# A fused attention and ReGLU block: half of one more norm transposed by DMA, one load moved forward, and a new order of steps

## The chip, the cores and the metric

The kernel runs on one core of a Trainium2 chip. The core has a matrix engine (PE, with its weight loads shown as PEld), a vector engine (DVE), a scalar engine (ACT), a small-work engine (POOL) and a queue engine (SP) that here only issues DMAs. Sixteen DMA engines move data. Each compute engine takes its instructions in the order in which the program lists them for it, and an instruction that needs another engine's result waits for a semaphore. The metric is the device time of one execution in microseconds, lower is better.

## What is computed

One transformer block on 2048 positions of 512 channels, in bf16:

```python
x = A_x
h = x + _A_ref(_layernorm(x, axis=-1), A_wqkv, A_wo)
h2 = h + _B_ref(_layernorm(h, axis=-1), B_W_gate, B_W_up, B_W_down)
```

`_A_ref` is attention with 32 heads of 16 channels. Each position looks at 8 earlier positions, 2 apart, its own included: q, k, v from `wqkv`, logits, softmax over the 8, weighted sum of v, product with `wo`. `_B_ref` is a gated layer with 1376 hidden channels: `relu(x W_gate) * (x W_up)`, then `W_down`. The norms have no weights.

## The kernel before

The positions are cut into 4 chunks of 512, each of 4 blocks of 128. For each chunk the kernel adds small steps to a plan: a step has an engine, an assumed duration, dependencies, the buffers that it takes, and a function that issues its instructions. The steps of one chunk are, in short:

- first norm: statistics of each block on DVE (`xst`, L420, and `xag`, L423), two small functions on ACT for the inverse deviation (`xrl`, L433, and `xre`, L437), the normalized row on DVE (`xxn`, L455, a tile `row`, of which there are 5), and its transpose into the chunk's tile `quad` (9 of them). A transpose is either four matmuls against an identity on PE (`xtp`, L484) followed by an eviction on ACT (`xte`, L500) or on DVE (`xtv`, L498), or one DMA transpose issued by SP (`xtd`, L473). The table `DMAT` lists which pairs of blocks go by DMA: `('h',2,0)` means second norm, chunk 2, the pair that begins at block 0. Chunk 0's first norm goes block by block.
- q, k and v: 12 steps of 4 matmuls of 128x512 (`qkv`, L525), evicted by ACT (L533). In chunk 0 the first four q/k steps are cut into halves of 256 columns (`qka` needs blocks 0 and 1, `qkc` all four).
- scores: 4 products of q with shifted k on DVE (`pr`, L572, 2.2 us each), summed by PE (`sc0` and `sc1`, L578), exponential on ACT (`ex`, L594), a mask on DVE in chunk 0 (L597), the sum over the 8 positions on PE (L611) and its inverse on ACT (L614, L617).
- weighted sum: attention weights spread by PE (`bc`, L639) and evicted by ACT (`be`, L645), 4 products with shifted v on DVE (`mu`, L660, 2.2 us each), summed in trees. In chunks 0 to 2 the first level of a tree is an accumulating DMA issued by POOL (L692), the others are on DVE (L663, L667, L686).
- output projection on PE (`wo`, L712; in chunk 0 the residual is added by PE too, L715), residual sum (L721 on ACT in chunk 0, L723 on DVE elsewhere), squares on ACT (`hsq`, L409), second norm with the same kinds of transposes (`htp`, `hte`, `htd`).
- gated layer: `mm`, L750, on PE; L754 and L757 on ACT; L770 on DVE; `dn`, L787, on PE; the last sum on DVE (L798), and the store issued by SP (L802).

What sets the order: `RANK` holds one number for each step, in the order in which steps are added. `Plan.order` sorts each engine's steps by that number. So every engine's list, SP's included, is fixed by `RANK` alone; a start time that the planner works out from assumed durations and assumed landing times (`load(...)`) decides which free buffer a step gets, and in what sequence the engines' lists are written out. No step overtakes another on its engine, on the chip either.

Loads are issued in `setup()`: x of chunk 0 in four pieces and the q/k weights in four pieces, by SP and ACT in turn; then x of chunk 1, the v weights, x of chunks 2 and 3, `wo`, `W_up`, `W_gate` and `W_down`, all by SP. Between them stand small copies on POOL into the next load's destination. Such a copy reads something that an earlier load brings, so the next load, which overwrites the copied element, is issued only after that earlier load has landed. Before PE has data it runs 44 small matmuls on a cleared tile (L374) and later 16 more (L382).

Of the kernel before, what the change touches and what calls it, by code (L numbers as in the profile page):

```python
# [15 lines left out]


RANK = [
    0, 1, 2, 3, 4, 5, 6, 7, 8, 9, 10, 11, 12, 13, 14, 15, 16, 18, 19, 24,
    26, 31, 32, 17, 20, 22, 23, 25, 29, 34, 35, 28, 33, 37, 39, 41, 45, 48, 21, 27,  # L20
    30, 36, 38, 42, 44, 46, 63, 74, 40, 56, 68, 49, 51, 54, 43, 60, 72, 53, 66, 65,
    77, 70, 83, 75, 80, 90, 92, 87, 114, 102, 110, 85, 105, 93, 104, 115, 125, 129, 78, 88,
    95, 99, 103, 183, 193, 202, 132, 143, 150, 156, 152, 106, 109, 116, 123, 119, 168, 181, 216, 220,
    224, 180, 188, 217, 223, 231, 187, 196, 226, 229, 234, 162, 172, 201, 205, 207, 237, 240, 239, 245,
    247, 251, 242, 248, 243, 246, 252, 256, 259, 263, 250, 254, 265, 266, 272, 278, 269, 276, 285, 275,
    283, 273, 280, 286, 318, 322, 292, 301, 304, 314, 313, 324, 341, 311, 325, 298, 303, 334, 338, 326,
    330, 346, 354, 360, 337, 355, 317, 353, 347, 358, 370, 329, 352, 340, 348, 332, 345, 294, 350, 356,
    361, 374, 343, 365, 372, 381, 351, 362, 413, 357, 368, 367, 386, 418, 400, 425, 460, 464, 417, 427,
    457, 467, 376, 434, 446, 466, 410, 429, 437, 668, 55, 61, 52, 57, 50, 58, 47, 59, 62, 64,
    67, 84, 73, 82, 86, 71, 81, 69, 79, 89, 166, 175, 122, 136, 111, 130, 137, 190, 91, 101,  # L30
    127, 173, 149, 179, 94, 96, 163, 213, 158, 170, 98, 107, 108, 167, 208, 197, 249, 257, 244, 235,
    255, 260, 264, 268, 274, 296, 279, 302, 309, 305, 310, 307, 287, 295, 290, 293, 300, 319, 328, 364,
    369, 315, 320, 359, 363, 335, 342, 380, 382, 327, 336, 373, 375, 389, 395, 387, 392, 396, 402, 393,
    399, 398, 401, 397, 403, 405, 409, 404, 407, 411, 412, 416, 419, 420, 423, 421, 428, 422, 426, 431,
    474, 482, 441, 443, 458, 463, 453, 468, 483, 438, 448, 436, 452, 442, 451, 450, 454, 456, 488, 492,
    479, 498, 455, 487, 491, 500, 507, 461, 493, 445, 459, 481, 485, 471, 475, 496, 511, 539, 524, 533,
    520, 535, 526, 530, 541, 514, 540, 484, 502, 543, 544, 556, 581, 589, 538, 552, 559, 562, 549, 554,
    584, 587, 529, 547, 560, 564, 113, 120, 100, 124, 76, 117, 97, 112, 128, 133, 140, 144, 142, 146,
    164, 145, 154, 148, 157, 161, 209, 230, 174, 186, 198, 200, 195, 215, 182, 184, 199, 228, 189, 211,
    169, 177, 178, 194, 232, 241, 271, 281, 185, 191, 261, 253, 284, 297, 289, 282, 308, 312, 321, 331,  # L40
    339, 344, 378, 366, 377, 371, 379, 383, 385, 394, 388, 391, 390, 430, 439, 470, 490, 424, 432, 473,
    476, 440, 447, 486, 489, 406, 415, 465, 477, 501, 518, 497, 504, 508, 512, 494, 499, 521, 525, 517,
    519, 516, 522, 503, 505, 527, 528, 532, 546, 534, 537, 536, 548, 531, 542, 579, 597, 566, 594, 585,
    601, 561, 580, 609, 599, 603, 588, 592, 571, 575, 577, 600, 605, 606, 610, 595, 623, 602, 611, 582,
    614, 627, 558, 576, 574, 578, 568, 572, 565, 567, 583, 621, 648, 639, 645, 636, 649, 591, 616, 652,
    624, 635, 628, 633, 640, 655, 663, 665, 667, 632, 654, 661, 711, 650, 656, 707, 710, 644, 657, 659,
    669, 126, 138, 118, 134, 131, 139, 121, 135, 141, 147, 155, 160, 151, 171, 159, 165, 153, 176, 203,
    236, 218, 225, 192, 204, 214, 219, 258, 291, 262, 270, 222, 233, 267, 277, 227, 238, 212, 221, 288,
    316, 206, 210, 306, 299, 323, 333, 384, 349, 408, 414, 433, 435, 444, 462, 449, 506, 510, 509, 513,
    515, 469, 495, 478, 472, 480, 563, 570, 586, 593, 523, 551, 557, 569, 573, 590, 596, 598, 545, 550,  # L50
    553, 555, 615, 622, 604, 607, 612, 619, 608, 613, 626, 629, 618, 620, 630, 631, 617, 625, 634, 637,
    638, 641, 646, 653, 643, 651, 642, 647, 691, 695, 681, 692, 694, 698, 688, 697, 700, 679, 687, 674,
    677, 670, 680, 666, 671, 690, 673, 675, 672, 682, 658, 662, 660, 678, 683, 684, 689, 664, 685, 699,
    702, 676, 693, 705, 701, 706, 704, 709, 686, 703, 708, 713, 715, 716, 718, 696, 714, 719, 720, 722,
    724, 731, 712, 726, 732, 734, 717, 725, 727, 730, 728, 733, 735, 737, 721, 723, 729, 736,
]


# [33 lines left out]
class Plan:  # L92
# [9 lines left out]
    def add(self, key, *a, **k):  # L102
        op = Op(*a, **k)
        op.key = key
        op.seq = len(self.ops)
        if RANK:
            op.prio = RANK[op.seq]
        self.ops.append(op)
        for b in set(op.take) | set(op.use):
            b.left += 1  # L110
        return op
# [76 lines left out]
def kernel(  # L188
# [11 lines left out]
    nc = tc.nc  # L200
# [4 lines left out]
    NT = D // P  # L205
# [11 lines left out]
    BPC = CS // P  # L217
# [4 lines left out]
    x_rows = A_x.rearrange("b (tb p) d -> p (b tb) d", p=P)  # L222
# [20 lines left out]
    x_sm = sb.tile([P, NTB, D], BF16, name="x_sm")  # L243
    wqk_sb = sb.tile([P, NT, 2 * D], BF16, name="wqk_sb")
    wv_sb = sb.tile([P, NT, D], BF16, name="wv_sb")
# [32 lines left out]
    def setup():  # L278
# [3 lines left out]
            (nc.scalar if j % 2 else nc.sync).dma_start(x_sm[:, j:j + 1, :], x_rows[:, j:j + 1, :])  # L282
        for dt in range(NT):
            (nc.scalar if dt % 2 else nc.sync).dma_start(wqk_sb[:, dt:dt + 1, :], w3_r[:, dt:dt + 1, 0:2 * D])
        nc.scalar.preload_act_table_set("natural_log_exp_and_others")
        V.memset(warm[:], 0.0)
        make_identity(nc, identity[:])
# [7 lines left out]
        nc.gpsimd.memset(vT[:, :, 0:PADL], 0.0)  # L295


        nc.gpsimd.tensor_copy(out=x_sm[0:1, BPC, 0:1], in_=x_sm[0:1, 0, 0:1])
        nc.sync.dma_start(x_sm[:, BPC:2 * BPC, :], x_rows[:, BPC:2 * BPC, :])
        nc.gpsimd.tensor_copy(out=wv_sb[0:1, 0, 0:1], in_=wqk_sb[0:1, NT - 1, 0:1])  # L300
        nc.sync.dma_start(wv_sb[:], w3_r[:, :, 2 * D:3 * D])
        nc.gpsimd.tensor_copy(out=x_sm[0:1, 2 * BPC, 0:1], in_=x_sm[0:1, BPC, 0:1])
        for tk in range(2, NCK):
# [32 lines left out]
    DAL = 5.5  # L336
    TDD, TDL = 1.25, 1.5
    NWARM, NFILL = 44, 8
    DMAT = (('h',2,0),('h',2,2),('x',3,0),('x',3,2),('h',3,0),('h',3,2),('h',1,0))

    EARLY = (1, 2, 3)

# [20 lines left out]
    def load(t):  # L363
        return add(None, "LD", 0.0, None, lat=t)

    xload = [[load(t) for t in (3.4, 3.4, 4.2, 4.2)]] + [[load(t)] * BPC for t in (9.5, 14.0, 15.5)]
    wload = {n: load(t) for n, t in
             (("q", 8.0), ("k", 8.0), ("v", 12.0), ("o", 17.5), ("u", 21.5), ("g", 25.5), ("d", 29.5))}

    wb = Buf(bank_s)  # L370

# [14 lines left out]
    def layernorm(tk, src, dst_slots, pr, groups, on_act, residual=None):  # L386
# [7 lines left out]
        for grp in groups:  # L394
# [72 lines left out]
            for j0 in range(lo, hi, step):  # L467
                if (ln, tk, j0) in DMAT:
                    for j in range(j0, min(j0 + step, hi)):
# [38 lines left out]
    for tk in range(NCK):  # L508
# [143 lines left out]
        for t in range(NT):  # L652
# [18 lines left out]
            if (tk, t) in PESUM:  # L671
                u = Buf(od_s)
# [66 lines left out]
        for f0 in range(0, NFT, 2):  # L739
# [3 lines left out]
            for ft in fts:  # L743
# [20 lines left out]
                d = add(("ge%d" % (f0 // 2), tk), "ACT", A5, f_ge, [c], pr - 200, take=[gr], use=[gm], lat=AL)  # L764
# [50 lines left out]
    with tc.manual_schedule():  # L815
        setup()
        for op in todo:
            if op.fn is not None:
                op.fn()
# [35 lines left out]
```

The softmax here doesn't subtract the row's maximum and nothing guards it: scores larger than these inputs give would overflow.

## Time and profile before

| | |
|---|---|
| median of 13 runs | 203.53 us (202.96 to 204.83) |
| the profiled execution | 203.53 us, of which the span of the profile is 201.6 us |
| granted PE clock | 0.999 of full speed |
| step of one 128x512 matmul, start to start | 0.216 us |
| DVE, product of q and k or of weights and v (128x4096) | 2.28 us, 32 of them |
| DVE, statistics of one block | 0.67 us, 16 of them |
| ACT, one eviction of 128x512 | 0.60 to 0.64 us |
| ACT, eviction of two transposed blocks (128x1024) | 1.03 us, 7 of them |
| SP, issue of one DMA transpose | 1.20 to 1.86 us, 14 of them; landing 2.4 to 4.9 us after the issue begins |
| x of one chunk (512 KB), issue to landing | 6.1 us (median of three) |

How to read the profile: its times run from the span's start. An instruction's busy time can overlap the next one's on the same engine, since the engines are pipelined; from start to start they stand a little closer than the busy time says. A row of the timeline gives the start, the time from the first start to the last end of the instructions merged in it, engine, line, operation, tiles and shape, and in brackets how long the engine was idle before it and which instruction or transfer ended that.

### The profile page before, as it was taken

Reading aid. Unit: us, or ns where it says so; the run is one execution under the profiler, and the core shown is the slowest. Engines: PE = TensorE matmul, PEld = TensorE weight load, DVE = VectorE, ACT = ScalarE, POOL = GpSimd, SP = SyncE. Lnnn points to the kernel's source line nnn. Section 1 sums busy time; section 2 is a strip of 40 time slices with the busy share of each in tenths; the row PEclk is TensorE's granted clock in tenths of the full one; section 3 lists DMA queues with packets and bytes.
Section 4 is the critical chain, followed back from the end, with each engine's and each line's share of the span. In section 5 each row is a group of like instructions: output and inputs, shape, how many; then the busy total and the mean of one; then the engine's idle time right before and its main releaser. Section 6 shows DMA issues by size and latency. Waiting matters only on the chain.

```text
span 201.6 us, 2940 instructions
## 1 busy us (share of the span) xinstructions
PE 193.8 (96%) x1095; PEld 96.3 (48%) x1115; DVE 153.2 (76%) x239; ACT 122.0 (61%) x256; POOL 12.9 (6%) x29
## 2 busy tenths in 40 slices
PE   8799999989999999999999999999999999999993
PEld 8686446545445434444444444444444444444452
DVE  6688999999999999999996958799967422122313
ACT  3358699746899966787536679801556731277500
POOL 4000000330000004100122000000000000000000
PEclk9999999999999999999999999999999999999999
DMA  5779971897000008930199600131010050200103
GB/s 150 266 235 393 402 232 29 157 201 137 3 0 0 0 3 156 189 71 3 29 179 194 147 3 0 26 78 52 3 52 0 0 104 3 78 0 0 52 0 104
DMA packets 17676, 18.81 MB, mean 93 GB/s; under 512 B 8352, under 2 KB 14464, under 8 KB 17664
## 3 DMA queue, kind: packets, MB, share of 16 engines
q1 hardware_dynamic: 15360, 11.57, 18.4%
q0 software_dynamic: 1728, 6.29, 16.8%
q10 hardware_dynamic: 576, 0.79, 1.5%
q8 instruction: 8, 0.13, 0.3%
q14 instruction: 4, 0.03, 0.1%
HBM read 8.42 MB, written 2.10 MB: 52 GB/s over the span
## 4 chain that ended last, share of the span: by engine, by line
PE 54%; DVE 24%; DMA 11%; ACT 5%; issue 2%; SPq 1%; POOL 0%; DVEq 0%; ACTq 0%; POOLq 0%
PE bank L750 29%; PE bank L787 14%; DMA x_sm<-in_A_x_dram 7%; DVE big L572 7%; DVE big L660 7%; PE bank L525 6%; PE bank L712 5%; DMA quad<-row 4%; DVE st L420 2%; DVE row L455 2%; DVE gT L770 2%; DVE x_sm L723 1%; DVE big L663 1%; ACT big L645 1%; ACT row L409 1%
## 5 line engine op out<-in xcount | busy, mean ns | idle before, releaser
L750 PE MATMUL bank<-quad,wu_sb 128*128 128x512 bf16 (+1 forms) x172 | 42.4, 379 | 0.4
L750 PE MATMUL bank<-quad,wg_sb 128*128 128x512 bf16 (+1 forms) x173 | 42.0, 379 | 0.3 <-DMA quad<-row 0.3
L757 ACT ACTIVATE gr<-bank 128x512 bf16<-128x512 f32 (+1 forms) x44 | 25.3, 616 | 24.7 <-PE bank L750 22.9
L787 PE MATMUL bank<-wd_sb,gT 128*128 128x512 bf16 (+2 forms) x183 | 39.8, 366 | 0.2
L754 ACT CAST up_sb<-bank 128x512 bf16<-128x512 f32 (+1 forms) x44 | 25.0, 600 | 21.0 <-PE bank L750 17.3
L572 DVE TENSOR_TENSOR big<-quad,kT 128x4096 bf16<-128x4096 bf16 x16 | 36.2, 2283 | 0.1
L660 DVE TENSOR_TENSOR big<-big,vT 128x4096 bf16<-128x4096 bf16 x16 | 35.9, 2282 | 0.0
L770 DVE TENSOR_TENSOR gT<-gr,up_sb 128x1024 bf16<-128x1024 bf16 (+1 forms) x24 | 15.3, 643 | 24.0 <-ACT up_sb L754 14.4
L525 PE MATMUL bank<-quad,wqk_sb 128*128 128x512 bf16 (+1 forms) x139 | 30.2, 355 | 1.9 <-DMA wqk_sb<-in_A_wqkv_dram 0.9
L787 PEld LDWEIGHTS <-gT 128*128 128x128 bf16 (+1 forms) x187 | 18.1, 98 | 19.6 <-issue 0.4
L750 PEld LDWEIGHTS <-wg_sb 128*128 128x128 bf16 (+1 forms) x176 | 17.3, 100 | 21.2 <-issue 0.9
L750 PEld LDWEIGHTS <-wu_sb 128*128 128x128 bf16 (+1 forms) x176 | 17.5, 100 | 20.6 <-issue 0.7
L525 PEld LDWEIGHTS <-wqk_sb 128*128 128x128 bf16 x144 | 15.5, 114 | 13.9 <-issue 2.2
L798 DVE TENSOR_TENSOR row<-x_sm,bank 128x512 bf16<-128x512 bf16 (+1 forms) x17 | 10.6, 650 | 10.4 <-PE bank L787 10.4
L645 ACT CAST big<-bank 128x512 bf16<-128x512 f32 x32 | 17.7, 635 | 0.3 <-PE bank L639 0.2
L663 DVE TENSOR_TENSOR big<-big 128x1024 bf16<-128x1024 bf16 (+2 forms) x24 | 16.8, 728 | 0.1
L692 POOL DMA_DIRECT2D big<-big x12 | 10.5, 875 | 87.7 <-DVE big L660 59.8
L525 PE MATMUL bank<-quad,wv_sb 128*128 128x512 bf16 x62 | 15.6, 380 | 0.2
L712 PE MATMUL bank<-wo_sb,quad 128*128 128x512 bf16 x62 | 15.2, 379 | 0.2
L455 DVE TENSOR_SCALAR row<-x_sm,mv,rs 128x512 bf16<-128x512 bf16 x32 | 11.4, 408 | 3.1 <-ACT rs L437 3.1
L500 ACT COPY quad<-bank 128x1024 bf16<-128x1024 bf16 (+1 forms) x9 | 8.0, 932 | 6.8 <-PE bank L484 6.8
L533 ACT CAST quad<-bank 128x512 bf16<-128x512 f32 x16 | 9.4, 608 | 4.5 <-PE bank L525 4.5
(69 smaller groups left out, 147.5 us busy)
## 6 DMA issues: line engine op xcount, KB each, us to landing
big<-big POOLq DMA_DIRECT2D x12, 512.0 KB, 5.3
out_dram<-row SPq DMA_DIRECT2D x15, 128.0 KB, 1.8
x_sm<-in_A_x_dram SPq DMA_DIRECT2D x3, 512.0 KB, 6.1
wu_sb<-in_B_W_up_dram SPq DMA_DIRECT2D x1, 1376.0 KB, 9.3
wg_sb<-in_B_W_gate_dram SPq DMA_DIRECT2D x1, 1376.0 KB, 12.3
wd_sb<-in_B_W_down_dram SPq DMA_DIRECT2D x1, 1280.0 KB, 16.4
wqk_sb<-in_A_wqkv_dram ACTq DMA_DIRECT2D x2, 256.0 KB, 6.6
wqk_sb<-in_A_wqkv_dram SPq DMA_DIRECT2D x2, 256.0 KB, 6.7
```

The source lines that it names most:

```text
L455: V.tensor_scalar(out=xn.t[:], in0=x, scalar1=mv.t[:, j, 0:1], scalar2=rs.t[:, j:j + 1], op0=ALU.add if residual else ALU.subtract, op1=AL ...
L525: nc.tensor.matmul(mm.t[:, lo:hi], lhsT=wv_sb[:, dt, t:D:NT] if c == 2 else wqk_sb[:, dt, c * D + t:(c + 1) * D:NT], rhs=xnT.t[:, dt, lo:h ...
L572: V.tensor_tensor(out=pb.t[:].rearrange("p (t w) s -> p t w s", t=2), in0=q4, in1=k4, op=ALU.mult)
L645: nc.scalar.copy(out=ab.t[:, w, :], in_=bc.t[:])
L660: V.tensor_tensor(out=mt.t[:], in0=ab.t[:], in1=v8, op=ALU.mult)
L663: V.tensor_tensor(out=mt.t[:, 0:n, :], in0=mt.t[:, 0:n, :], in1=mt.t[:, n:2 * n, :], op=ALU.add)
L712: nc.tensor.matmul(od.t[:], lhsT=OT.t[:, t, j * P:(j + 1) * P], rhs=wo_sb[:, t, :], start=(t == 0), stop=(t == NT - 1 and tk not in RPE))
L750: nc.tensor.matmul(mm.t[:fs, :], lhsT=w_sb[:, dt, ft * P: ft * P + fs], rhs=hnT.t[:, dt, :], start=(dt == 0), stop=(dt == NT - 1))
L754: nc.scalar.copy(out=ub.t[:fs, i, :], in_=um.t[:fs, :])
L757: nc.scalar.activation(out=gr.t[:fs, i, :], in_=gm.t[:fs, :], func=ACT.Relu)
L770: V.tensor_tensor(out=gt.t[:fs, 0:n, :], in0=gr.t[:fs, 0:n, :], in1=ub.t[:fs, 0:n, :], op=ALU.mult)
L787: nc.tensor.matmul(od.t[:, c0:c1], lhsT=gts[ft].t[:fs, ft % 2, j * P:(j + 1) * P], rhs=wd_sb[:fs, ft, c0:c1], start=(ft == 0), stop=(ft == ...
```

## The change

1. `DMAT` gets `('x',2,2)`: in the first norm of chunk 2, blocks 2 and 3 are transposed by DMA (two more issues on SP), and no longer by 8 matmuls on PE and one eviction on ACT. Blocks 0 and 1 of that norm stay on PE. The order of entries in the table has no meaning.
2. x of chunk 1 is issued by SP right after the q/k weights, without a POOL copy ahead of it. The copy ahead of the v weights now reads x of chunk 0, block 0, instead of the last piece of the q/k weights. The loads behind are issued in the same order, x of chunk 2 still after the landing of x of chunk 1.
3. The planner's assumed landing times of x of chunks 1 to 3 and of the v weights are 0.5 to 1.0 us smaller.
4. `RANK` is another permutation, of 737 steps instead of 738, so the order changes on every engine. Some of what that does in the built program: on DVE the first statistics of chunk 1 stand ahead of chunk 0's last normalized row; on PE chunk 0 begins with `qka0`, `qka2`, then the transposes of blocks 3 and 2, then `qka1` and `qka3`; on SP two transposes of chunk 2 stand ahead of chunk 3's four; one of chunk 1's score steps stands ahead of chunk 0's output projection, the other behind it, where both stood behind it before.

The diff, the table of numbers left out (in the changed file the lines after 300 stand one line higher):

```diff
 RANK = [
...
 ]
@@
         for dt in range(NT):
             (nc.scalar if dt % 2 else nc.sync).dma_start(wqk_sb[:, dt:dt + 1, :], w3_r[:, dt:dt + 1, 0:2 * D])
+        nc.sync.dma_start(x_sm[:, BPC:2 * BPC, :], x_rows[:, BPC:2 * BPC, :])
         nc.scalar.preload_act_table_set("natural_log_exp_and_others")
@@
-        nc.gpsimd.tensor_copy(out=x_sm[0:1, BPC, 0:1], in_=x_sm[0:1, 0, 0:1])
-        nc.sync.dma_start(x_sm[:, BPC:2 * BPC, :], x_rows[:, BPC:2 * BPC, :])
-        nc.gpsimd.tensor_copy(out=wv_sb[0:1, 0, 0:1], in_=wqk_sb[0:1, NT - 1, 0:1])
+        nc.gpsimd.tensor_copy(out=wv_sb[0:1, 0, 0:1], in_=x_sm[0:1, 0, 0:1])
         nc.sync.dma_start(wv_sb[:], w3_r[:, :, 2 * D:3 * D])
         nc.gpsimd.tensor_copy(out=x_sm[0:1, 2 * BPC, 0:1], in_=x_sm[0:1, BPC, 0:1])
@@
-    DMAT = (('h',2,0),('h',2,2),('x',3,0),('x',3,2),('h',3,0),('h',3,2),('h',1,0))
+    DMAT = (('h',2,0),('h',2,2),('h',3,0),('h',3,2),('x',3,0),('x',3,2),('x',2,2),('h',1,0))
@@
-    xload = [[load(t) for t in (3.4, 3.4, 4.2, 4.2)]] + [[load(t)] * BPC for t in (9.5, 14.0, 15.5)]
+    xload = [[load(t) for t in (3.4, 3.4, 4.2, 4.2)]] + [[load(t)] * BPC for t in (8.5, 13.5, 15.0)]
     wload = {n: load(t) for n, t in
-             (("q", 8.0), ("k", 8.0), ("v", 12.0), ("o", 17.5), ("u", 21.5), ("g", 25.5), ("d", 29.5))}
+             (("q", 8.0), ("k", 8.0), ("v", 11.5), ("o", 17.5), ("u", 21.5), ("g", 25.5), ("d", 29.5))}
```

## The prediction

> **What bounds the kernel now.** First the engines' busy time, then who waits for whom on PE. (The profiled execution took 203.53 us, which is also the median of the 13 runs, with 201.6 us of span and 1.9 us around it; my sum is made against it.)
>
> ```profile
> PE 193.8 (96%) x1095; PEld 96.3 (48%) x1115; DVE 153.2 (76%) x239; ACT 122.0 (61%) x256; POOL 12.9 (6%) x29
> ```
>
> ```profile
> PE bank L525 <- DMA wqk_sb<-in_A_wqkv_dram: 0.9, 1, 0.9
> PE bank L525 <- DMA quad<-row: 0.7, 1, 0.7
> ...
> PE bank L750 <- DMA quad<-row: 0.3, 1, 0.3
> ```
>
> PE has three holes after its warm-up: for the q/k weights (until 9.34), for the last DMA transpose of chunk 3's first norm (until 41.75), and for the second DMA transpose of chunk 1's second norm (until 104.77). Start to start, where a step of one matmul is 0.216, the last two lose 0.88 and 0.46. So removing PE work saves nothing unless what these waits hang on comes earlier too. Busy time by stretch (columns: length, then PE, PEld, DVE, ACT, POOL) says what that is:
>
> ```profile
> 62.00:99.00 37.00, 36.69 (x233) 16.14 (x235) 36.86 (x46) 30.42 (x63) 3.78 (x5) 1.00 0.31 58
> 42.00:62.00 20.00, 19.89 (x115) 9.81 (x116) 19.09 (x23) 15.11 (x37) 0.86 (x1) 1.00 0.36 67
> 105.00:198.00 93.00, 92.52 (x438) 43.32 (x445) 53.90 (x94) 45.88 (x95) 1.72 (x2) 1.00 0.19 45
> ```
>
> From 62 to 99 DVE is as full as PE (36.86 of 37), and its rows L455 feed the transposes that end the hole at 104.77. After 105 only PE counts. The chain of waits names the transfers:
>
> ```profile
> 3.76 6.77 DMA x_sm<-in_A_x_dram
> ...
> 36.67 4.94 DMA quad<-row
> ...
> 101.23 3.40 DMA quad<-row
> ```
>
> **The load moved.** x of chunk 1 is issued some 1.1 us earlier (SP ended its weight issues at 2.60 and issued it at 3.76), and wv, until now issued at 9.35, at about 3.8. Does x of chunk 1 land earlier than 3.76 + 6.77 = 10.53? The DMA share by stretch (the column before the last):
>
> ```profile
> 7.00:8.00 1.00, 0.94 (x17) 0.76 (x14) 0.96 (x5) 0.89 (x4) 0.00 (x0) 1.00 0.97 354
> ...
> 9.00:10.00 1.00, 0.66 (x8) 0.66 (x9) 0.00 (x0) 0.00 (x0) 0.18 (x1) 1.00 0.27 97
> ...
> 14.00:15.00 1.00, 1.00 (x7) 0.52 (x5) 1.00 (x4) 1.00 (x3) 0.00 (x0) 1.00 1.07 369
> ```
>
> Until 8 the 16 engines are full with x and q/k weights that stand ahead of it; then most are done and a quarter (0.27) go on until 10.53. One engine's 32 KB of a 512 KB load take 1.4 us (369 / 16 = 23 GB/s), and the weights' last part let PE go at 9.34 (POOL saw it at 9.14): 9.1 + 1.4 = 10.5. The landing is that of the late engines, set by what stands ahead, not by the issue. Bounds: 9.1 if no engine were late, 10.7 if wv disturbed a little. I take 10.5. The gain that the move does bring is that wv fills the idle 9 to 11 us; x of chunk 2 stays gated by chunk 1's landing but finds no wv ahead (landing near 15 instead of 16.06). POOL has one gate copy fewer (0.18), on no path.
>
> [...]
>
> **The new wait on DVE.** In the changed program's DVE order the first statistics of chunk 1 (L420) stand before the last normalized row of chunk 0 (block 2) and before the second copy L498; before, they stood behind both.
>
> ```profile
> 7.55 0.82 DVE L455 TENSOR_SCALAR row<-x_sm,mv,rs 128x512 bf16<-128x512 bf16 x2
> 10.01 0.42 DVE L498 COPY quad<-bank 128x512 bf16<-128x512 bf16 x1 [1.63 <-PE bank L484]
> 10.56 2.47 DVE L420 BATCH_NORM_STATS2 st<-x_sm 128x6 f32<-128x512 bf16 x4
> ...
> 13.91 1.38 DVE L455 TENSOR_SCALAR row<-x_sm,mv,rs 128x512 bf16<-128x512 bf16 x4 [0.60 <-ACT rs L437]
> 16.08 0.69 DVE L420 BATCH_NORM_STATS2 st<-x_sm 128x6 f32<-128x512 bf16 x1 [0.79 <-DMA x_sm<-in_A_x_dram]
> ```
>
> The row that ended near 8.4 now waits for the landing: statistics from 10.56, 0.59 to the next instruction (2.47 less 0.69, over 3), 11.15, the row 0.41, 11.56. PE sees it at 11.61. PE's own time:
>
> ```profile
> 9.34 0.41 PE L525 MATMUL bank<-quad,wqk_sb 128*128 128x256 bf16 x2 [0.87 <-DMA wqk_sb<-in_A_wqkv_dram]
> 9.58 0.39 PE L484 MATMUL bank<-identity,row 128*128 128x128 bf16 x4
> ...
> 16.54 1.06 PE L484 MATMUL bank<-identity,row 128*128 128x128 bf16 x16
> ```
>
> From 9.34 it has the rest of one half step (0.22), another (0.43) and block 3's transposes (0.22): 10.22. Then it waits until 11.61: **a new hole of 1.39** where PE ran without one from 9.34 to 16.54. Behind the waiting transposes stand all of chunk 0's other q/k steps, so chunk 1's transposes begin at 17.93. If x landed by 9.14 the hole would be nothing.
>
> [...]
>
> **DVE up to the rows of chunk 3.** Chunk 1's rows start 0.33 + 0.35 (row and copy now in between) later, 14.6, end at 15.9, and the wait of 0.79 for x of chunk 2 goes; the work up to 33 is the same. One new wait: the mask of the second half needs scores whose PE step runs 1.39 late (28.25 instead of 26.86; 1.11 to the exponential, 0.6 for it: ready 30.0, DVE there at 29.7). And chunk 3's rows need an L437 that ACT now runs behind one of the evictions L645 of that step, 32.2 against 31.7 before. So its rows end near 33.5 instead of 33.0.
>
> **The transposes by DMA.** Half of chunk 2's first norm leaves PE: 8 transposes, 0.45 (30.91 to the next step at 31.36), and one eviction of 1.03 on ACT, which has idle time there. SP issues two more; one row is early, the other comes at 32.05, and an issue takes 1.2 to 1.3, so chunk 3's four start near 33.4, 34.7, 36.0 and 37.25 (before 32.7 to 36.67). The last lands 4.9 later, as before, because the accumulating DMAs L692 start then too: 42.2, PE goes at **42.33 instead of 41.75**. Its own arrival is 40.87 + 1.39 - 0.45 = 41.81, so 0.5 of a hole stays. Chunk 2's own landing, 32.1 + 2.5, is before its first step at 36.2.
>
> **From there to 105.** Before chunk 0's output projection (L712) PE now runs one of chunk 1's score steps L578 (1.08 with its change of shape); 11 steps of 0.863 + 1.08 + 2 of 0.863 after 42.33 is 54.6 (before 52.97). ACT's L721, L409 and the two small functions follow PE: the last of them ends near 63.0, before 61.73, so the rows L455 of chunk 0's second norm start at 63.05 instead of 61.93: **DVE is 1.1 late as it enters the stretch where it has no idle time.** Nothing there gives it back but the gate product ahead of chunk 1's rows, now the 96-row one (0.33 for 0.60): +0.85. The transposes by DMA and the hole's end move by as much: 104.77 + 0.85 = 105.6; PE would be there at 104.31 + 0.58 = 104.9. After it PE has the same matmuls. In the new order the four-transpose norms of chunks 2 and 3 have 12.3 and 13.8 us of PE work between their last L712 and their first L750 (before 13.8 and 13.0, of which some 11.7 were used): no new hole; the tail is as before. **Sum: 203.53 + 0.85 = 204.4.**
>
> **Rivals.**
> 1. Late engines are not late, x lands near 9.1 (for: three quarters of the engines are done then; against: the rows above). The hole at 10.2 goes and DVE is 1.3 earlier, but the score step ahead of L712 keeps the gain small: PE starts chunk 3 near 41.0 by the transposes, the rows L455 start at 61.75, and 104.77 becomes 104.3: 203.1. Break-even with before at a landing of 9.6, since the time follows the landing by about 0.9.
> 2. Faster: x lands by 9.14 and DVE runs the whole way through ahead of PE, so that both old holes close. The mechanism is PE alone: 0.45 + 0.88 + 0.46 = 1.8, 201.7. It decides only if DVE's rows before 99 come 0.9 earlier than PE's saving asks; DVE's 0.14 of idle time from 62 to 99 speaks against it.
> 3. Worse: the orders of ACT and PE fit each other only at the assumed times; one more hole of the first kind (an eviction behind a late L437, a bank not free), carried whole: 204.4 + 0.9 = 205.3.
>
> **How the numbers follow.** Main case 0.54 (its own range 203.9 to 204.9), rival 1 0.20, rival 2 0.13, rival 3 0.13. Predicted 204.4. The range 202.8 to 205.2 leaves out rival 2 and the upper part of rival 3. A change under 0.3% (0.6 us) can't be told from none, so slower begins at 204.14: main 0.47 and rival 3 give 0.60; same: most of rival 1 and the main case's rest, 0.25; faster: rival 2 and a little of rival 1, 0.15.
>
> **What would show it.** Right: an idle time of 1.2 to 1.5 on PE near 10.2, released by DVE's L455; statistics from 10.5; PE's wait for the quad transposes ending near 42.3 and near 105.6; DVE without idle time from 63 to 99. Wrong: x of chunk 1 landing near 9, no hole at 10.2, or the hole near 105 gone.

## The result and the profile after

| | before | after |
|---|---|---|
| median | 203.45 us (48 runs, 202.0 to 205.35) | 205.58 us (11 runs, 205.08 to 207.23) |
| ratio, 95% interval (the medians alone give 1.0105) | | 1.0125 (1.0101 to 1.0148) |
| the profiled execution, its span | 203.53, 201.6 | 205.47, 203.7 |

Slower, as forecast, but by 2.1 us and not 0.9: above the range's end of 205.2. First the page's busy times of the changed kernel:

```profile
PE 193.8 (95%) x1087; PEld 96.3 (47%) x1107; DVE 153.1 (75%) x239; ACT 121.9 (60%) x255; POOL 12.7 (6%) x28
```

The 8 transposes are gone from PE (1095 to 1087), and its time is the same. Its waits (us in total, times, longest):

```profile
PE bank L483 <- DVE row L454: 1.4, 1, 1.4
...
PE bank L749 <- DMA quad<-row: 0.6, 1, 0.6
PE bank L524 <- DMA quad<-row: 0.5, 1, 0.5
```

The first is new. The others are the two old holes: 0.5 for chunk 3's first norm (0.7 before), 0.6 for chunk 1's second norm (0.3 before). Timeline of PE, then of DVE, in the changed kernel:

```profile
9.08 0.85 PE L524 MATMUL bank<-quad,wqk_sb 128*128 128x256 bf16 x6 [0.81 <-DMA wqk_sb<-in_A_wqkv_dram]
9.76 0.39 PE L483 MATMUL bank<-identity,row 128*128 128x128 bf16 x4
11.51 0.40 PE L483 MATMUL bank<-identity,row 128*128 128x128 bf16 x4 [1.36 <-DVE row L454]
```

```profile
7.75 0.38 DVE L454 TENSOR_SCALAR row<-x_sm,mv,rs 128x512 bf16<-128x512 bf16 x1
10.45 0.69 DVE L419 BATCH_NORM_STATS2 st<-x_sm 128x6 f32<-128x512 bf16 x1 [2.32 <-DMA x_sm<-in_A_x_dram]
11.06 0.40 DVE L454 TENSOR_SCALAR row<-x_sm,mv,rs 128x512 bf16<-128x512 bf16 x1
...
14.46 1.39 DVE L454 TENSOR_SCALAR row<-x_sm,mv,rs 128x512 bf16<-128x512 bf16 x4 [0.60 <-ACT rs L436]
15.75 1.87 DVE L419 BATCH_NORM_STATS2 st<-x_sm 128x6 f32<-128x512 bf16 x3
```

DVE idles 2.32 for x of chunk 1, with chunk 0's row queued behind, and PE idles 1.36 for that row. The wait for x of chunk 2 (0.79 before) is gone. The transfers in the chain of waits:

```profile
0.73 2.60 DMA x_sm<-in_A_x_dram
3.36 7.07 DMA x_sm<-in_A_x_dram
...
37.28 4.96 DMA quad<-row
...
101.70 4.39 DMA quad<-row
```

x of chunk 1 was issued 0.40 earlier (3.36, as the first piece of x landed) and lands at 10.43, 0.1 earlier. By stretch (length, PE, PEld, DVE, ACT, POOL, clock, DMA share, GB/s):

```profile
9.00:10.00 1.00, 0.92 (x10) 0.89 (x10) 0.00 (x0) 0.00 (x0) 0.00 (x0) 1.00 1.09 377
10.00:11.00 1.00, 0.15 (x3) 0.00 (x0) 0.55 (x1) 0.00 (x0) 0.18 (x1) 1.00 0.56 181
...
62.00:99.00 37.00, 36.47 (x231) 16.26 (x234) 36.15 (x44) 31.19 (x64) 3.45 (x4) 1.00 0.30 58
```

wv fills the DMA engines at 9 to 10 (0.27 before, 1.09 now), and at 10 to 11 PE has nothing to do. DVE is still nearly full from 62 to 99 (0.61 of its idle time there is the wait for the first row of chunk 0's second norm). DVE, POOL and PE at three places, first in before, then after:

```profile
98.67 0.86 POOL L692 DMA_DIRECT2D big<-big  x1 [15.88 <-DVE big L660]
104.77 1.02 PE L750 MATMUL bank<-quad,wg_sb 128*128 128x512 bf16 x4 [0.29 <-DMA quad<-row]
```

```profile
63.17 1.38 DVE L454 TENSOR_SCALAR row<-x_sm,mv,rs 128x512 bf16<-128x512 bf16 x4 [0.61 <-ACT rs L436]
99.99 0.86 POOL L691 DMA_DIRECT2D big<-big  x1 [15.53 <-DVE big L659]
106.13 1.04 PE L749 MATMUL bank<-quad,wg_sb 128*128 128x512 bf16 x4 [0.64 <-DMA quad<-row]
```

Milestones in us, from the timelines and the records of stores:

| | before | after | difference |
|---|---|---|---|
| chunk 3's q, k, v begin | 41.75 | 42.37 | 0.62 |
| first row of chunk 0's second norm | 61.93 | 63.17 | 1.24 |
| POOL's accumulating DMA (L692, now L691) ahead of the last hole | 98.67 | 99.99 | 1.32 |
| hole's end | 104.77 | 106.13 | 1.36 |
| last matmul's start | 197.98 | 199.36 | 1.38 |
| last store landed | 200.64 | 201.94 | 1.30 |
| end of the span | 201.60 | 203.70 | 2.10 |

So there are two losses: 1.36 by the hole's end, and 0.8 behind the last store. Four of the 11 executions took 206.5 to 207.2, all with a mean granted clock of 0.992 (the other seven have a median of 205.42); of the 114 executions of before that ran beside the experiments none was under 0.994.

### The profile page after: what moved, and what is told of

It is laid out like the page before. It is cut to its first block, busy times and chain, and to the rows that moved or that the text cites. A ratio compares the mean times of both kernels' runs of the same rounds, so it can differ in the third digit from the quotient of the medians.

```text
span 203.7 us, 2939 instructions
## 1 busy us (share of the span) xinstructions
PE 193.8 (95%) x1087; PEld 96.3 (47%) x1107; DVE 153.1 (75%) x239; ACT 121.9 (60%) x255; POOL 12.7 (6%) x28
## 4 chain that ended last, share of the span: by engine, by line
PE 65%; DVE 16%; DMA 9%; ACT 4%; issue 3%; ACTq 0%; DVEq 0%
PE bank L749 30%; PE bank L786 14%; PE bank L524 13%; DVE big L659 7%; DMA x_sm<-in_A_x_dram 5%; PE bank L711 5%; DMA quad<-row 5%; DVE big L571 3%; PE bank L577 2%; DVE gT L769 2%; DVE row L454 1%; DVE big L662 1%; ACT row L408 1%; DVE x_sm L722 1%; ACT quad L499 1%
## 5 line engine op out<-in xcount | busy, mean ns | idle before, releaser
L786 PE MATMUL bank<-wd_sb,gT 128*128 128x512 bf16 (+3 forms) x184 | 39.4, 366 | 0.2
L691 POOL DMA_DIRECT2D big<-big x12 | 10.5, 875 | 88.5 <-DVE big L659 62.7
L419 DVE BATCH_NORM_STATS2 st<-x_sm 128x6 f32<-128x512 bf16 x16 | 10.5, 681 | 2.7 <-DMA x_sm<-in_A_x_dram 2.7
L532 ACT CAST vT<-bank 128x512 bf16<-128x512 f32 x16 | 9.5, 608 | 4.4 <-PE bank L524 4.2
```

Source lines behind the costliest of these rows:

```text
L786: nc.tensor.matmul(od.t[:, c0:c1], lhsT=gts[ft].t[:fs, ft % 2, j * P:(j + 1) * P], rhs=wd_sb[:fs, ft, c0:c1], start=(ft == 0), stop=(ft == ...
```

## The experiments

Each is compared with the kernel before on its own chip (203.32 to 203.51). "Hole's end" is that near 105. "Theory" and "rival" are the names that an expectation gives to the explanations it sets against each other.

**The row on VectorE, put back.** After, with

```diff
+RANK[35], RANK[44], RANK[212], RANK[210] = RANK[212], RANK[35], RANK[210], RANK[44]
```

> The changed kernel with one edit: on DVE chunk 0's last normalized row and its second copy go ahead of chunk 1's first statistics again; the order of all other engines, the loads and the transposes stay. Theory A (the row behind the waiting statistics is the start of the loss): the hole of 1.36 on PE near 10 goes, chunk 1's rows start some 0.65 earlier, PE starts chunk 3 near 41.2 instead of 42.37, and the step that waits near 106 starts some 1.1 earlier; 0.9 to 1.3 us less than the changed kernel, still slower than before, as the end from the last store's landing to the end of the span (1.76 us, before 0.96) stays. Theory B (the rest of the new order costs it, above all the score step ahead of the output projection): under 0.4 us less. Theory C (the two more DMA transposes cost it): under 0.4 us less, PE still waits until about 42.

204.60 (ratio 1.0061, 1.0033 to 1.0090), 1.0 less than the changed kernel: theory A by the time. In its profile chunk 3 begins at 41.78 and the hole ends at 105.54, each 0.6 earlier and not 1.1, but the q/k weights came 0.29 later there. PE's timeline has no hole between the two blocks' transposes:

```profile
9.37 0.84 PE L524 MATMUL bank<-quad,wqk_sb 128*128 128x256 bf16 x6 [1.02 <-DMA wqk_sb<-in_A_wqkv_dram]
10.05 0.61 PE L483 MATMUL bank<-identity,row 128*128 128x128 bf16 x8
10.50 2.77 PE L524 MATMUL bank<-quad,wqk_sb 128*128 128x256 bf16 x19
```

**The same row, moved behind in the kernel before.** Before, with the two first statistics ahead of row and copy:

```diff
+RANK[216], RANK[35], RANK[214], RANK[44] = RANK[35], RANK[44], RANK[216], RANK[214]
```

> The kernel before with one thing of the change: in the order of VectorE's work chunk 1's first two statistics stand ahead of chunk 0's last normalized row and its second copy; every other engine's order, the loads and the number of DMAs are those of before. Theory R (the moved row is about 1.0 us of the 2.1): a hole of 1.3 to 1.5 us in TensorE's work near 10 us, all later milestones 0.7 to 1.1 later, the median 204.2 to 204.6, some executions with a granted clock of 0.992 and 1.8 us more. Rival A (VectorE's old wait of 2.2 us for x of chunk 1 and 2 takes it up, and the row costs only together with the new loads): the hole is there, but chunk 3 starts within 0.2 of 41.7 and the median is 203.3 to 203.7.

204.73 (1.0070, 1.0039 to 1.0100): the row costs 1.3 here, a little more than theory R said, and 2 of 12 executions had a clock of 0.992. The hole on PE:

```profile
11.12 0.40 PE L484 MATMUL bank<-identity,row 128*128 128x128 bf16 x4 [1.19 <-DVE row L455]
```

So the row is shown from both sides, taken out and put in.

**The loads alone.** Before, with the change's three lines on loads.

> The kernel before with the changed kernel's loads alone (x of chunk 1 without a gate, the v weights gated by x of chunk 0). Theory A (the landing of x of chunk 1 is set by the weights ahead of it): it lands at 10.3 to 10.6 as before (10.53), x of chunk 2 lands near 14.2 instead of 16.06, DVE's wait of 0.79 goes; 0 to 0.6 us less than before. Rival (the v weights disturb the q/k weights): PE's first wait for weights ends after 9.6 instead of 9.34, 0.3 us more than before or worse. Rival 2: x of chunk 1 lands near 9 and DVE gains 1.3.

203.62 (1.0020, 0.9995 to 1.0044). Chunk 2's statistics begin at 15.12 and not 16.08, yet chunk 3 begins at 41.68 (41.75 before): no gain in time.

**The half alone.** Before, with `('x',2,2)` in `DMAT`, and the first six stores cut into 64 rows each.

> The kernel before with the half of chunk 2's first norm transposed by DMA and nothing else of the change; six early stores of the output are cut in two, so that the last stores use the same five semaphores as in before (tail of 0.9 to 1.0). Theory H (the half is worth nothing: TensorE has 0.45 us less work, but chunk 3's rows and its own columns come later): chunk 3 starts at 41.4 to 42.3, hole's end within 0.3 of 104.8, median 203.0 to 203.7. Rival G (the 0.45 us comes off the end): median 202.7 to 203.0. Rival L (the transposes in one queue make chunk 3 late): median 203.9 or more.

204.11 (1.0040, 1.0018 to 1.0062): by the time theory L, 0.7 more than before. DVE's timeline:

```profile
28.97 2.33 DVE L455 TENSOR_SCALAR row<-x_sm,mv,rs 128x512 bf16<-128x512 bf16 x7
32.66 0.41 DVE L455 TENSOR_SCALAR row<-x_sm,mv,rs 128x512 bf16<-128x512 bf16 x1 [1.36 <-DMA quad<-row]
```

The eighth row waits 1.36 for a DMA transpose: the `row` buffers are five, and one of them is taken again only as a transfer out of it lands. In the changed order that wait is absent. This profile is of an early execution, the fastest of the 12 (chunk 1's statistics at 9.36; 10.56 in before's profile), and chunk 3 still begins at 41.79: what PE saves goes into its wait there, 1.95 instead of 0.71. Where the slower executions lose the 0.7 this profile does not show.

**The score step, put back on TensorE alone.** After, with `RANK[256] = RANK[260] - 0.5`.

> The changed kernel with one step moved on TensorE: the first score step of chunk 1 stands behind chunk 0's four output projections again, next to the second score step, as in before. Theory S (the score step ahead of the projections is worth 0.3 to 0.9): the first row of chunk 0's second norm comes at 62.3 to 62.9 and not at 63.2, the hole's end at 105.3 to 105.8 and not at 106.1, the median 204.7 to 205.2. Rival Z (the score step is worth nothing, the rows are late because all of VectorE's queue is): first row within 0.2 of 63.2, hole's end within 0.2 of 106.1, median 205.4 to 205.7.

209.66, neither theory. The step's exponential kept its place on ACT, ahead of the residual reads, so ACT and then PE waited (ACT's timeline, then PE's):

```profile
61.89 0.60 ACT L593 ACTIVATE ex<-bank 128x512 bf16<-128x512 f32 x1 [4.87 <-PE bank L577]
```

```profile
67.65 0.38 PE L610 MATMUL bank<-ex,same 128*128 128x512 bf16 x1 [2.88 <-ACT ex L593]
```

It measures a fault of the edit, not the step. The run below held the same edit and fell with it, 208.99, with the same two waits (4.87 and 2.9):

> The changed kernel with the three suspects put back together: the row and the copy of chunk 0 ahead of chunk 1's statistics, the first score step behind the projections, and six early stores cut in two so that the last stores use the semaphores of before. What stays of the change: the loads, the half, the rest of the searched order. Theory T (these three are the whole loss): tail 0.9 to 1.0, hole's end 104.6 to 105.1, median 203.0 to 203.7, the same as before. Rival U (the rest of the order costs too): median 204.0 or more, hole's end 105.3 or later.

**The score step with its exponential.** After, with

```diff
+RANK[256], RANK[257] = RANK[260] - 0.5, RANK[261] - 0.5
```

> The changed kernel with chunk 1's first score step behind the output projections on TensorE, and now with its exponential moved along on ScalarE, next to the second exponential, so that ScalarE's residual reads don't stand behind it. Theory S (the score step ahead of the projections is worth 0.3 to 0.9): first row of chunk 0's second norm at 62.2 to 62.9 (63.17 in the changed kernel), hole's end at 105.3 to 105.8 (106.13), median 204.7 to 205.2. Rival Z (worth nothing: the squares on ScalarE or VectorE's queue set it): within 0.2 of 63.17 and 106.13, median 205.4 to 205.7.

205.17 (1.0103, 1.0077 to 1.0129; two of six executions at 0.987 and 0.988). The first row of chunk 0's second norm comes at 62.23 (63.17 in the changed kernel). From chunk 3's beginning to the hole's end it is 63.15; 63.76 in the changed kernel, 63.02 in before. So 0.4 to 0.6, theory S.

**The end of the program.** The prediction had nothing for the 0.8. In the traces of before and of the changed kernel SP ends with the same list of nine waits (118, 100, 102, 104 to 109); the DMAs that SP and ACT issue signal their landing on eight semaphores in turn (100, 102, 104 to 109), and those of the last five stores, 105 to 109 in before, are 107, 108, 109, 100 and 102 in the changed kernel, with its two DMAs more. Two runs shift that turn: `W_up` and `W_gate` in halves in before (two DMAs more), in quarters in after (six more).

> The kernel before with the loads of W_up and W_gate in two halves each: two more DMAs on SP, as the change makes two more, and nothing else. The last store of all then signals on the same semaphore as in the changed kernel, which SP's closing list of waits names early. Theory D (SP walks its closing list of waits in a fixed order, so a last store that signals on an early one leaves the rest of the walk behind its landing): from the last landing to the end of the span 1.6 to 1.8 us instead of 0.96, the last DVE instruction as before: 0.6 to 0.9 us more than before. Rival (the longer end comes from something else, such as the fetching of instructions at another place of the program): 0.2 us or less.

> The changed kernel with the loads of W_up and W_gate in four pieces each: six more DMAs on SP, so that the last store signals on the semaphore that the closing list names last, as in the kernel before. Theory D: from the last landing to the end 0.9 to 1.0 us instead of 1.76; 0.6 to 0.9 us less than the changed kernel. Rival: no difference beyond 0.2 us; or the six more issues delay later loads, and PE waits for weights.

The first took 204.0 (1.0046, 1.0020 to 1.0072), 0.6 more than before, with 1.84 from landing to end: theory D. The second had 0.89 from landing to end, as expected, but no gain: it took 207.28, in part by the clock (next), and its one execution at full clock took 205.47, as long as the changed kernel's. Counted from the last matmul, its end is no shorter (us, from the traces; "sum" is DVE's last):

| | end of the sum to issue of the last store | end of the sum to its landing | landing to the end | last matmul's start to the end |
|---|---|---|---|---|
| before | 0.33 | 1.93 | 0.96 | 3.62 |
| after | 0.26 | 1.85 | 1.75 | 4.34 |
| before, halves | 0.34 | 1.93 | 1.84 | 4.50 |
| after, quarters | 0.69 | 2.76 | 0.89 | 4.38 |

The list of SP's semaphore records in the traces says why (us from the last landing, semaphores waited for; the second row is of the run with the stop moved, below):

```
after       0.02 102/115  0.09 104/114  0.16 105/113  0.63 106/112  0.72 107/111  0.79 108/101  0.86 109/110  0.93 drain ... 1.75 end
stop moved  -1.14 118/117  -0.65 100/116  -0.57 102/115 ... 0.02 109/110  0.08 drain ... 0.91 end
```

In the changed kernel the landing on 102 finds six more waits to be walked, 0.07 each, and among them a stop of 0.45. That stop stands behind SP's 79th recorded instruction in all 18 profiles, whatever that instruction is. (In before it comes 0.15 after the landing, where it delays the end by 0.07.) With quarters the 79th instruction is the wait just ahead of the last store's DMA, so the stop delays that store. DVE's last sum and the last store's issue, in the changed kernel, then with quarters:

```profile
199.67 0.42 DVE L797 TENSOR_TENSOR row<-x_sm,bank 128x256 bf16<-128x256 bf16 x1 [0.24 <-PE bank L786]
200.35 0.40 SPq L801 DMA_DIRECT2D out_dram<-row  x1
```

```profile
201.68 0.42 DVE L797 TENSOR_TENSOR row<-x_sm,bank 128x256 bf16<-128x256 bf16 x1 [0.24 <-PE bank L786]
202.79 0.33 SPq L801 DMA_DIRECT2D out_dram<-row  x1
```

The transfer itself then takes 2.06 instead of 1.59, for a reason that no run shows. So what the quarters gain behind the landing they lose ahead of it. Two last runs test the stop.

**The clock.** Granted clock by stretch in the run with quarters:

```profile
11.00:12.00 1.00, 0.28 (x5) 0.29 (x6) 1.00 (x3) 0.00 (x0) 0.00 (x0) 1.00 0.10 33
12.00:13.00 1.00, 1.00 (x9) 0.72 (x7) 1.00 (x3) 0.59 (x1) 0.00 (x0) 0.51 0.77 232
13.00:14.00 1.00, 1.00 (x5) 0.56 (x4) 1.00 (x6) 0.00 (x0) 0.00 (x0) 0.50 1.08 381
14.00:15.00 1.00, 0.78 (x3) 0.43 (x3) 0.39 (x3) 0.50 (x2) 0.00 (x0) 0.50 1.09 374
15.00:16.00 1.00, 1.00 (x8) 0.70 (x7) 1.00 (x5) 0.00 (x0) 0.00 (x0) 0.79 0.94 234
```

Half the clock from 12.0 to 15.4: (0.49 + 0.50 + 0.50 + 0.21) / 0.5 = 3.4 us, 1.7 us of work late. In the two expectations below "window" is such a stretch at half the clock. Then two runs put 22 small matmuls into the hole, in the changed kernel and in that with quarters:

```diff
+for _ in range(22 if tk == 0 and not residual and j == 2 else 0):
+    nc.tensor.matmul(tp.t[:, 0:P], lhsT=warm[:], rhs=warm[:], start=True, stop=True)
```

> The changed kernel with 22 small matmuls of the cleared tile ahead of the transposes of chunk 0's block 2 (some 1.2 us of TensorE work into the same bank, overwritten by the transposes), in the hole that waits for the row. They change no order. Theory C (in about a third of the executions of the changed kernel this hole makes the clock gate halve the clock for one window, 0.992 on the mean and 1.5 to 1.8 us): no execution at 0.992, none above 206.2, median 205.0 to 205.5. Rival E (the window goes by the hole before it, at 8.0 to 9.1, or by nothing in the kernel): about a third of the executions still at 0.992 and near 207.

> The changed kernel with the up and gate weights loaded in quarters, in which 5 of 6 executions had a mean granted clock of 0.992 and took 207.1 to 207.6, now with the 22 small matmuls in the hole ahead of block 2's transposes. Theory C (this hole decides the gate's window): at most 1 of the executions at 0.992, median 204.7 to 205.7. Rival E (the weight loads in quarters or the earlier hole did it): most executions still at 0.992 and near 207.3.

205.69 (205.58 to 205.79, 5 runs) and 205.77 (205.59 to 206.24, 6 runs), so with the hole filled the quarters make no difference. Theory C by the clock: with the hole open 9 of 17 executions were at 0.992 (4 of 11 and 5 of 6), with it filled none of 11. The row behind in before gave 2 of 12; the row put back still 1 of 11, with only the hole for the weights. Why the quarters have more of them than the changed kernel no run shows. PE's timeline of the first:

```profile
10.04 1.39 PE L482 MATMUL bank<-warm 128*128 128x128 bf16 x22
11.67 0.40 PE L485 MATMUL bank<-identity,row 128*128 128x128 bf16 x4 [0.24 <-DVE row L454]
```

The other seven executions of the changed kernel have a median of 205.42, and both medians here lie above what theory C said: the fill takes away the long executions and otherwise gains nothing, since the row comes no earlier.

**Put back together.** After with row, score step and exponential back, and the six stores cut; then after with row back and the half on PE; then with all of these back (no stores cut).

> The changed kernel with three things put back: the row and the copy of chunk 0 ahead of chunk 1's statistics on VectorE, the score step with its exponential behind the projections, and six early stores cut in two so that the last stores use the semaphores of before (tail 0.9 to 1.0). The loads, the half and the rest of the order stay. Theory T (row 1.0, tail 0.8, score step 0 to 0.5, and little else): 203.3 to 203.9. Rival U (something else in the order costs as well): 204.2 or more with the hole's end at 105.2 or later.

> The changed kernel with the row and the copy of chunk 0 ahead of chunk 1's statistics, and with blocks 2 and 3 of chunk 2's first norm transposed by TensorE as before. Two DMAs fewer, so the last stores use the semaphores of before (tail 0.9 to 1.0). The new loads and the rest of the order stay. Theory H (the half costs 0.4 to 0.8 by itself, as alone in before): 205.6 - 1.0 - 0.8 - 0.4 to 0.8 = 203.0 to 203.4. Rival F (in this order, which gives the transposes their row early, the half is free or a gain): 203.6 to 204.2.

> The changed kernel with everything put back that an earlier run showed to cost: row and copy ahead of the statistics, score step and exponential behind the projections, blocks 2 and 3 of chunk 2's first norm on TensorE (two DMAs fewer, so the last stores use the semaphores of before). The new loads and the rest of the order stay. Theory H (the half costs 0.2 to 0.7 in this order too): 203.1 to 203.6, no slower than before. Rival F (the half is free here, what is left of 0.45 over before is the rest of the order): 203.7 to 204.0, the same as with the half.

203.82 (1.0022, 1.0005 to 1.0040), 203.97 (1.0017, 0.9999 to 1.0035), 203.64 (1.0014, 0.9984 to 1.0044). All three come within 0.6 of before, and none has before's end: from the last matmul's start to the end their profiles have 4.24, 4.01 and 4.03 (before 3.62). The first has 0.89 from landing to end, but the stop delays its last store as with quarters; in the other two the last store signals on 109 again, but the stop stands behind the wait for it, so that 1.42 and 1.44 follow the landing and not the 0.9 to 1.0 expected. So theory T's median came out with nearly the whole loss at the end still in it, and the second's median lies in theory F's range, which was worked out with a short end.

With the end taken off (median less the profile's end, an estimate) the first and third both have 199.6, and before has 199.8: row and score step are the rest of the loss. The same estimate gives the row put back alone 200.3 and the second 200.0. So in this order the half costs 0.0 to 0.3, which is within the noise.

**The stop moved.** The third of these with the first eight stores cut in two, and that third once more beside it.

> The kernel of the run before (row, score step, exponential and half put back) with eight early stores cut in two: eight more instructions on SP, the last stores still on the semaphores of before. In all profiles so far SP stops for 0.43 to 0.48 us behind the 79th of its recorded instructions. Theory P (the stop sits at that place in SP's list): here it falls behind the first of the nine closing waits, ahead of the last landing, so it costs nothing; the time from the last landing to the end is 0.9 and not 1.44, the median 203.0 to 203.3. Rival Q (the stop comes with the closing of the program wherever that is): 1.3 to 1.5 stay, median 203.5 to 203.8.

> The kernel before this change of stores once more, for the comparison on the same chip: 203.4 to 203.9, 1.4 from the last landing to the end.

202.85 (0.9963, 0.9933 to 0.9992) beside 203.45 (0.9998): 0.6 by eight instructions on SP, theory P. The stop stands behind the first of the closing waits, at -1.14 to -0.65 in the list above, where SP would wait anyway; from the last matmul's start to the end it is 3.49, beside 4.01. So with row, score step, end and half put right nothing of the loss is left: this version is 0.4% (0.1% to 0.7%) faster than before, and 1.3% faster than the changed kernel.

## Why the prediction was wrong

1. **The new wait on DVE** was right: a hole of 1.36 (1.39 said), DVE's statistics at 10.45, the landing at 10.43 (10.5). Taking it out gives 1.0, putting it into before costs 1.3. That the issue would be 1.1 earlier was wrong (0.4): it is the ninth DMA, on the semaphore of the first piece of x, and SP waited for that to land. Nothing hung on it.
2. **Chunk 3's start** came at 42.37 (42.33 said). That the two added transposes set it is half right: with the row put back chunk 3 begins at 41.78 with the half still on DMA, so the late row is nearly all of the 0.62.
3. **The score step** was right as a mechanism and in its size up to the rows (63.17; 63.05 said). Putting it back gives 0.4 to 0.6.
4. **"Nothing there gives it back but the gate product ... +0.85"** was mis-sized: 1.36. DVE was 1.24 late at the first row and not 1.1. The 96-row product does bring the later rows forward (99.95, only 1.06 later), and the last transpose is issued only 0.47 later, but it takes 4.39 instead of 3.40. The hole's end follows the accumulating DMA, 1.32 later: in ten profiles it comes 6.0 to 6.3 after that DMA's issue, whatever the rows did (104.77 - 98.67 = 6.10 before, 106.13 - 99.99 = 6.14 after). No run moved the DMA alone, so that it is the cause is argued, not shown.
5. **"The tail is as before"** is the step that failed: 0.8 of the missing 1.3. I had followed PE to its last matmul and counted the two added DMA issues as 1.2 to 1.3 us of SP each, but not what they do to SP's closing list: six waits and a stop of 0.45 behind the last landing. Shown by the halves in before, where two DMAs more alone cost 0.6, and by the stop moved, which alone gives 0.6 back. The quarters don't show it: they take the waits out of the end, and the stop delays the last store instead.
6. **The clock.** The sum has nothing for it: that a hole of 1.39 leaves the granted clock at 1.00, as the hole of 0.87 does in before's profile, was my estimate, and the runs went against it. 4 of 11 executions had the clock of 0.992; they are 1.1 to 1.8 longer than the median of the others, near the 1.7 that the half-clock stretch of the run with quarters puts late. From 8.60 to 12.00, as long as that stretch and just ahead of it, PE is busy 2.61 of 3.40 in before, 1.56 in after, 1.44 with quarters, 2.82 filled, and executions at 0.992 or below are 0 of 114, 4 of 11, 5 of 6 and 0 of 5. But with the row put back, busy 2.58 in its profile, 1 of 11 was at 0.992 too. What sets the clock is not shown: that the holes together count, and not the longest alone, is argued, and the fill closes the longest hole as well.

The rivals: x of chunk 1 landing at 9.1 did not happen, and DVE did not run ahead of PE. The third, one more loss of some 0.9 carried to the end, came near the time (205.3) by luck: the loss lay at a place it did not name.

## What to carry to other kernels

Follow a change to the last instruction of the program: here two added DMAs turned the semaphores of the last stores and shifted SP's list, and each of the two cost some 0.4 us (six waits of 0.07, a stop of 0.45) where nothing is computed any more. Count an end from the last computation, not from the last landing: with quarters the landing itself came late, 2.76 behind the last sum and not 1.85. When a step is moved, its followers on other engines must move too: the score step took 209.66 without its exponential, 205.17 with it. Don't take a hole for harmless because it is short: with holes of 0.81 and 1.36 close together 4 of 11 executions here were at a clock of 0.992, with the longer one filled none of 5, and only the spread of the executions showed it, not the profiled one.

## What was not expected of the hardware

- SP stops for 0.44 to 0.48 us behind its 79th recorded instruction, in every kernel here, 81 to 94 instructions long. What it does then is not shown.
- A wait already met cost SP 0.06 to 0.08 us in the closing lists of before and of the changed kernel, nine waits long in both.
- Where the half alone went by DMA, DVE waited 1.36 for a row buffer, of which there are five, until a DMA transpose out of it had landed.
